# Three output buffers for narrowed weights, later routing gates, and the fixed-address token group last

## The chip, the cores and the metric

The kernel runs on one core of a Trainium2 chip. The time is the device time of one launch in microseconds (us), the median of three runs; the profile is of one further execution of the same program. The core's engines run side by side and meet through semaphores: PE multiplies matrices, DVE and ACT work on vectors, POOL does small vector work, and SP mostly issues DMA transfers. Each engine takes its instructions in the order in which they were written.

## The reference

Three layers run one after the other on 4 batches of 576 tokens, in float32:

```python
scores = scale * np.matmul(q, k.transpose(0, 1, 3, 2)) + bias      # 8 heads of 64
attn = exp(scores - max) / (sum + 1e-09)
x = (attn @ v) as [2304, 512]

e_idx = np.argmax(x @ w_gate, axis=1)                               # one of 8 experts per token
for e in range(E):                                                  # 512 -> 1024 -> 512
    out[mask] = gate_w * eom * (np.maximum(x[mask] @ w1[e], 0.0) @ w2[e])

g, val = x @ w_gate, x @ w_val                                      # 512 -> 1536
out = (g * sigmoid(g) * val) @ w_out                                # 1536 -> 512
```

## The kernel before

The program has three parts. In the first (to about 300 us) the attention of 16 units (four head pairs by four batches) fills the tiles `xT[0]` to `xT[3]`, each 128 rows by 2304 columns, one 576-column stretch per batch.

In the second (about 300 to 560 us) the expert layer is written as 64 steps, 16 per batch. Step n issues `h_step(n+1)` (12 matmuls, L590, evicted by ACT L592 and DVE L593), then `y_step(n)` (12 matmuls, L603, which read what L592 and L593 wrote), and then the side work that tables put at that step: `at(n, f)` and `after(n, f)` (L1047, L1086) collect it, and the loop at L1169 writes it out. An engine never overtakes, so side work that waits holds up whatever stands behind it on the same engine. Each batch is first run through its first expert; a packed list of leftover tokens then goes through one more expert. That list comes from the `q_` functions: `q_meta` (L624) loads the gate values of the chosen expert by DMA, `q_keep` (L640) marks tokens on DVE (L644 to L647), `q_rank` ranks them, `q_load` (L635) loads their `x` (L638), `q_tok` (L661) transposes it on PE (L666) and copies it on ACT (L667) into the buffer that held the layer's output `yo`. `QN` (L42) gives their steps. `x_save` (L617) writes a batch's `x` to DRAM (L619). The transfer `x<-yo` (L1142) writes a batch's result.

Side work also prepares the third layer's weights. They arrive as 64-bit values, and a "stash" reads one piece of 128x1024 words into one of three `xT` tiles (L982 or L984, three steps ahead), narrows it with one ACT instruction (L993) and three DVE instructions (L996, L999, L1002) into an output buffer in `xT[2]`, and stores it to the DRAM tensor `wn` (L1039). `NS` lists the steps of its 18 pieces, `NS2` those that spread over two steps.

In the third part (from about 560 us) the dense layer passes over three token groups of 768 columns, j = 0, 1, 2, in 12 steps each. Each pass ends with six result tiles o(h, m) of 128x512 in PSUM, copied to SBUF by DVE (L1552) or ACT (L1554) and sent to DRAM by SP (L1556). Two of the groups consist of batches whose numbers are only known at run time (`r0`, `r1`, `r2`), so their addresses are registers; the third (batch 3 and the last 64 tokens of every batch) has fixed addresses. The order of the groups is 0, fixed, 1 before the change. `ld_x` (L1471) loads the next group's input. SP's transfers count up eight semaphores in turn (DMAHW0 to 7 in the rows below), and a transfer waits for the one eight places earlier on its own semaphore. Two transfers to register addresses of the same DRAM tensor are also ordered by a wait, since the program cannot know that they do not overlap.

Of the kernel before, what the change touches and what calls it, by code (L numbers as in the profile page):

```python
# [13 lines left out]
AF = mybir.ActivationFunctionType  # L14
# [21 lines left out]
PR = {0: 72, 1: 73, 5: 75}  # L36
EB = 4
N0, NPL = 6, 6
NS = (9, 10, 13, 18, 19, 20, 21, 24, 25, 29, 34, 35, 37, 39, 40, 41, 43, 49)
NS2 = (13, 29, 37, 43)  # L40
RT = (3, 4, 5, 5, 6, 7, 7)
QN = (43, 46, 44, 46, 49, 54, 56)  # L42
EL, EC = ((47, 51, 53), (50, 51, 52, 53, 55, 56))
QT, SX = (44, 2)
SP0 = (10, 12, 14, 16, 17)
# [68 lines left out]
def body(tc, qt, kt, va, vb, ws, moe_w_gate, moe_w_output_gate, moe_w1, moe_w2, w_gate, w_val, w_out, ctab, cst, cst2, out):  # L114
    nc = tc.nc
    with ExitStack() as ctx:
# [39 lines left out]
        for r in range(4):  # L156
            o = slice(32 * r, 32 * r + 32)
# [7 lines left out]
        xT = {}  # L165
# [448 lines left out]
        def x_src(p, b):  # L614
            return xT[p][:, b * S:b * S + S]

        def x_save(b):  # L617
            for p in range(NP):
                nc.sync.dma_start(x1[p, :, b], x_src(p, b))  # L619
# [280 lines left out]
        for n, (ui, c) in enumerate(steps):  # L900
            p, b = units[ui]
# [28 lines left out]
            if old:  # L930
                x = pS.tile([128, 2, 512], F32, tag="S", name="Tx") if c == 4 else None
                t = t_pe(old[3], old[4], x, sts[ui - 1] if ui else None)
# [87 lines left out]
            return xT[(0, 1, 3)[i % 3]].bitcast(I32)[:, 0:1024]  # L1020

        def s_out(i):
            return xT[2][:, 512 * (i % 2):512 * (i % 2) + 512]

        def stash(i, n, m, two):

# [14 lines left out]
        def stash_ld(i, n, m):  # L1041
            at(m - 3, lambda: fetch_w(n, s_raw(i)))
# [43 lines left out]
        def at(n, *fs):  # L1086
            todo.setdefault(n, []).extend(fs)
        at(QN[0], q_meta)
        at(QT, lambda: xq.update(T=nc.values_load(lst[0:1, 64:65], min_val=0, max_val=28)))
# [3 lines left out]
        at(QY, lambda: x_first(1))  # L1093
        at(QN[1], q_load)
        at(QN[2], q_keep)
        at(QN[3], q_rank)
        for c in range(5):
            at(QN[4] + c, q_tok(c))
        at(QN[5], q_gather)
        at(QN[6], q_selt)  # L1100
        for i in range(N0 // 2):
            at(EL[i], lambda i=i: early_ld(i))
        for n in range(N0):
            for i, f in enumerate(early_cv(n)):
                at(EC[n] + i + (n == 3 and i == 2), f)
        for i, m in enumerate(NS):
            stash(i, 3 * NPL + i, m, m in NS2)
        for i, m in enumerate(NS):
            stash_ld(i, 3 * NPL + i, m)
# [11 lines left out]
            at(F1[f - 5], lambda f=f: m_load_f(0, f))  # L1121
        at(3, lambda: m_gate(0))
        for b in range(B):
            at((4, 5, 28, 30)[b], lambda b=b: x_save(b))
        for b in range(1, B):
            n = 16 * b - 15
            for i, f in enumerate(mu[b]["sp"]):
# [16 lines left out]
        a, z = prev  # L1144
        t = t_pe(a[3], a[4], None)
# [13 lines left out]
        t = t_pe(z[3], z[4], None)  # L1159
# [9 lines left out]
        for n in range(16 * B):  # L1169
            b, s = divmod(n, 16)  # L1170
# [204 lines left out]
        with ExitStack() as c2:  # L1375
# [140 lines left out]
            def rows(j, h, m):  # L1516

                def dst(b, c):
                    return of[bass.ds(b, 1) if not isinstance(b, int) else slice(b, b + 1), 0:512].rearrange("o (p c) d -> c p (o d)", c=4)[c]
                if j == 0:  # L1520
                    return [(0, 128, dst(r0, 2 * h + m) if m < 2 else dst(r1, h))]
                if j == 1:
                    return [(0, 128, dst(r2, 2 * h + m - 1) if m else dst(r1, 2 + h))]
                if m:
                    return [(0, 128, dst(3, 2 * h + m - 1))]
                return [(32 * b, 32, of[b, 512 + 32 * h:544 + 32 * h]) for b in range(B)]

            def outs(n, h, m):
                j, f = steps[n]
                first, last = n % NF == 0, n % NF == NF - 1  # L1530
                if first:
                    ops[h, m] = po.tile([128, 512], F32, tag=f"o{h}{m}", name="o")
                t = ops[h, m]
                uh, ul = (u[:, 128 * m:128 * m + 128] for u in sv[n]["u"][h])
                oh, ol = wt[f][2]
                for i, (u, w) in enumerate(((uh, oh), (uh, ol), (ul, oh))):
                    nc.tensor.matmul(t, u, w, start=first and i == 0, stop=last and i == 2)  # L1537
                if last:
                    end = j == 2
                    if end:  # L1540
                        o = sv["end"][:, 512 * (3 * h + m):512 * (3 * h + m) + 512]
                    else:
                        o = wp.tile([128, DM], F32, tag="ot", bufs=3, name="ot")
                    parts = rows((0, 2, 1)[j], h, m)
                    if end and (h, m) == (1, 2):
                        nc.vector.tensor_copy(o[:, 0:256], t[:, 0:256])  # L1546
                        nc.scalar.activation(o[:, 256:512], t[:, 256:512], AF.Copy)  # L1547
                        nc.sync.dma_start(parts[0][2][:, 0:256], o[:, 0:256])
                        nc.sync.dma_start(parts[0][2][:, 256:512], o[:, 256:512])
                        return  # L1550
                    if m % 2 == 0:
                        nc.vector.tensor_copy(o, t)  # L1552
                    else:
                        nc.scalar.activation(o, t, AF.Copy)  # L1554
                    for a, c, dst in parts:
                        nc.sync.dma_start(dst, o[a:a + c])  # L1556

            def it(n):

                N = len(steps)  # L1560
                j, f = steps[n] if n < N else (3, 0)
                i = n % NF
# [94 lines left out]
                F("h")  # L1657
                O(1, 2)
                if j < 2 and i == NPL + (j == 0):
                    ld_x(2 - j)  # L1660

            for n in range(6, 9):
                n_load(n)
# [23 lines left out]
```

## Time and profile before

| what | value |
|---|---|
| median of the runs shown (lowest to highest) | 992.91 us (992.63 to 994.26) |
| profiled execution: its own time, its span | 994.33 us, 992.4 us |
| PE busy, share of span | 953.1 us, 96% |
| DVE, ACT, POOL busy | 694.2, 532.0, 115.9 us |
| mean granted TensorE clock | 0.991 |
| moved by DMA, mean rate | 130.26 MB, 131 GB/s |

The span runs from the first to the last instruction; the execution's own time is 1.9 us longer. PE is the engine with least idle time, so what counts is where PE waits, where its clock was granted at half (1.2 instead of 2.4 GHz), and what follows its last matmul.

### The profile page before, as it was taken

How to read it: one execution, taken by the hardware profiler on the slowest of the kernel's cores; microseconds unless marked ns; L12 is line 12 of the kernel's file. 1: busy time of each engine (PE TensorE's matmuls, PEld its weight loads, DVE VectorE, ACT ScalarE, POOL GpSimd, SP SyncE). 2: the span in 40 equal slices, each digit the busy share in tenths (PEclk: the TensorE clock that was granted, in tenths of full speed). 3: DMA queues.
4: the chain of work that ended last, by engine and by line, in shares of the span. 5: the costliest groups of instructions: out<-in, count | busy, mean ns of one | idle time of the engine just before them, and what ended most of it. 6: DMA issues, size and time to landing. Idle time of an engine off the chain costs nothing. (4 is left out here: it accounts for less than half of the span.)

```text
span 992.4 us, 19678 instructions
## 1 busy us (share of the span) xinstructions
PE 953.1 (96%) x7633; PEld 813.4 (82%) x7633; DVE 694.2 (70%) x1548; ACT 532.0 (54%) x1125; POOL 115.9 (12%) x116
## 2 busy tenths in 40 slices
PE   7979999999999999999899999999999999999994
PEld 2337777777768999999899899999999999999993
DVE  8977888877786676677456577777556677367652
ACT  6778777777775343534335444554434455244441
POOL 2673434343300000000000000000000000000000
PEclk9999999999999999999999999999999999999997
DMA  6785334333044473947745585420312300312101
GB/s 203 206 258 172 124 92 130 97 114 112 2 143 154 144 266 121 373 150 234 252 135 200 169 258 180 118 75 1 127 32 84 109 33 22 107 53 75 64 1 64
DMA packets 90271, 130.26 MB, mean 131 GB/s; under 512 B 13728, under 2 KB 48032, under 8 KB 90176
## 3 DMA queue, kind: packets, MB, share of 16 engines
q1 hardware_dynamic: 90176, 128.99, 40.5%
q8 instruction: 60, 0.98, 0.4%
q14 instruction: 35, 0.29, 0.1%
HBM read 93.50 MB, written 35.46 MB: 130 GB/s over the span
## 5 line engine op out<-in xcount | busy, mean ns | idle before, releaser
L272 DVE CUSTOM_DVE_ANT_0 E<-S,bias 128x576 f32<-128x576 f32 x128 | 91.8, 755 | 31.2 <-PE S L268 25.1
L277 ACT ACTIVATE E<-E,st 128x576 f32<-128x576 f32 x144 | 110.3, 769 | 4.2 <-DVE st L272 3.9
L1275 PE MATMUL Y<-fv,ws 128*128 128x384 f32 x540 | 108.8, 336 | 0.1
L1275 PEld LDWEIGHTS Y<-fv,ws 128*128 128x128 f32 x540 | 95.7, 188 | 3.2 <-issue 0.4
L268 PEld LDWEIGHTS S<-kh,qz 64*128 64x128 f32 (+1 forms) x576 | 56.1, 185 | 39.2 <-DVE st L272 22.0
L379 PE MATMUL pv<-pt,rawv 128*64 128x320 f32 (+1 forms) x576 | 88.1, 422 | 0.0
L268 PE MATMUL S<-kh,qz 64*128 64x288 f32 (+1 forms) x576 | 82.0, 320 | 4.6 <-DVE st L272 3.4
L1537 PE MATMUL o<-ws,u 128*128 128x512 f32 x306 | 84.1, 394 | 0.0
L1016 DVE TENSOR_TENSOR ws<-r,ws 128x512 fp32r<-128x512 f32 (+1 forms) x66 | 51.4, 779 | 32.0 <-ACT ws L1013 31.1
L1275 PE MATMUL X<-fr,ws 128*128 128x384 f32 x360 | 73.3, 338 | 0.0
L592 ACT ACTIVATE qz<-T 128x288 fp32r<-128x288 f32 x63 | 25.8, 409 | 88.2 <-PE T L590 87.2
L318 ACT ACTIVATE pt<-T 128x512 f32<-128x512 f32 (+3 forms) x112 | 50.7, 467 | 38.6 <-PE T L295 38.2
L1275 PEld LDWEIGHTS X<-fr,ws 128*128 128x128 f32 x360 | 65.0, 188 | 5.6
L1537 PEld LDWEIGHTS o<-ws,u 128*128 128x128 f32 x306 | 56.2, 187 | 6.6 <-DVE u L1330 0.4
L603 PE MATMUL y<-qz,w2hl 128*128 128x288 f32 x384 | 57.8, 300 | 3.5 <-DVE qz L593 1.7
L603 PE MATMUL y<-qz,whl 128*128 128x288 f32 x384 | 56.9, 296 | 1.6 <-DVE qz L593 1.6
L320 DVE COPY pt<-T 128x512 f32<-128x512 f32 (+3 forms) x112 | 55.8, 522 | 3.3 <-PE T L295 3.1
L603 PEld LDWEIGHTS y<-qz,w2hl 128*128 128x128 f32 x384 | 53.7, 191 | 4.7 <-ACT qz L592 2.7
L590 PE MATMUL T<-xh,whl 128*128 128x288 f32 x256 | 57.1, 298 | 0.0
L590 PE MATMUL T<-xh,w1hl 128*128 128x288 f32 x248 | 55.7, 300 | 0.0
L295 PE MATMUL T<-ident,E 64*128 64x64 f32 x1248 | 54.5, 222 | 0.0
L603 PEld LDWEIGHTS y<-qz,whl 128*128 128x128 f32 x384 | 52.8, 188 | 2.1 <-DVE qz L593 2.1
(314 smaller groups left out, 2099.8 us busy)
## 6 DMA issues: line engine op xcount, KB each, us to landing
r<-wn SPq DMA_DIRECT2D x22, 512.0 KB, 3.5
bscr<-ob SPq DMA_DIRECT2D x36, 288.0 KB, 3.7
bias<-bscr SPq DMA_DIRECT2D x14, 576.0 KB, 4.3
raww<-in_moe_w_dram SPq DMA_DIRECT2D x10, 768.0 KB, 7.3
raww<-in_moe_w_dram SPq DMA_DIRECT2D x14, 512.0 KB, 5.8
raww<-in_moe_w_dram SPq DMA_DIRECT2D x22, 256.0 KB, 4.2
ro<-wn SPq DMA_DIRECT2D x22, 256.0 KB, 2.6
rawq<-in_qt_dram SPq DMA_DIRECT2D x16, 320.0 KB, 3.0
```

The costliest lines, as they stand in the source:

```text
L268: nc.tensor.matmul(t[:, f, 0:288], x[k, a], y[k, o], start=i == 0, stop=i == 2)
L272: nc.vector.tensor_tensor_reduce(out=E.rearrange("p (a b) -> p a b", a=2), in0=ps[:, :, 0:288], in1=bt[p, hh, c].rearrange("p (a b) -> p a ...
L277: nc.scalar.activation(E, E, AF.Exp, bias=st[:, 2 * c + hh:2 * c + hh + 1], scale=-1.0, accum_out=st[:, 10 + 2 * c + hh:11 + 2 * c + hh])
L295: nc.tensor.transpose(t[r][:, at:at + 64], E[k, o:o + 128], ident[k, k])
L318: nc.scalar.activation(o, x, AF.Copy)
L320: nc.vector.tensor_copy(o, x)
L379: nc.tensor.matmul(st["ps"][64 * hh:64 * hh + 64, 0:w], vt[p][:, hh, b, c, :], y, start=c == order[0], stop=c == order[4])
L590: nc.tensor.matmul(ps, wa[:, x, k], xs[k][y][:, o], start=k == 0 and i == 0, stop=k == 3 and i == 2)
L603: nc.tensor.matmul(hbuf["y"][d // 2][:, d % 2, 0:288], wb[:, x, d], t[:, y:y + 288], start=f == 0 and i == 0, stop=(one or f == 7) and i == 2)
L1016: return lambda: eng.tensor_tensor(l, t, h.bitcast(F32), ALU.subtract)
L1275: nc.tensor.matmul(bank, a[:, c], x[:, k], start=first and k == 0 and n == 0, stop=k == 1 and n == 2, skip_group_check=True)
L1537: nc.tensor.matmul(t, u, w, start=first and i == 0, stop=last and i == 2)
```

## The change

- The passes of the third part take the token groups in the order 0, 1, fixed: the `rows((0, 2, 1)[j], ...)` at L1544 becomes `rows(j, ...)`, and `ld_x(2 - j)` becomes `ld_x(j + 1)`.
- In the last pass DVE copies o(0,0), o(0,2), o(1,0) and o(1,1), and ACT copies o(0,1); before, DVE copied o(0,0), o(0,2), o(1,0) and ACT o(0,1), o(1,1). o(1,2) stays split in halves. The transfers of that pass go out partly on SP, partly on ACT: thirteen of them (eight of 32 rows), six on ACT.
- From piece 8 on, the stash takes three output buffers in turn, the third at columns 1152 to 1664 of `xT[2]`, where batch 2 lay.
- The stash list loses step 49 and gains step 26, so that pieces 9 to 17 move to an earlier place in the list.
- `x_save` of batches 2 and 3 stands at steps 22 and 33 (before 28 and 30).
- `q_keep` stands at step 45 (before 44).

```diff
-NS = (9, 10, 13, 18, 19, 20, 21, 24, 25, 29, 34, 35, 37, 39, 40, 41, 43, 49)
+NS = (9, 10, 13, 18, 19, 20, 21, 24, 25, 26, 29, 34, 35, 37, 39, 40, 41, 43)
-QN = (43, 46, 44, 46, 49, 54, 56)
+QN = (43, 46, 45, 46, 49, 54, 56)
...
         def s_out(i):
-            return xT[2][:, 512 * (i % 2):512 * (i % 2) + 512]
+            o = 512 * (i % 2) if i < 8 else (0, 512, 1152)[i % 3]
+            return xT[2][:, o:o + 512]
...
-            at((4, 5, 28, 30)[b], lambda b=b: x_save(b))
+            at((4, 5, 22, 33)[b], lambda b=b: x_save(b))
...
-                    parts = rows((0, 2, 1)[j], h, m)
+                    parts = rows(j, h, m)
                     if end and (h, m) == (1, 2):
                         nc.vector.tensor_copy(o[:, 0:256], t[:, 0:256])
                         nc.scalar.activation(o[:, 256:512], t[:, 256:512], AF.Copy)
                         nc.sync.dma_start(parts[0][2][:, 0:256], o[:, 0:256])
-                        nc.sync.dma_start(parts[0][2][:, 256:512], o[:, 256:512])
+                        nc.scalar.dma_start(parts[0][2][:, 256:512], o[:, 256:512])
                         return
-                    if m % 2 == 0:
+                    if (h, m) == (0, 1) or m == 1 and not end:
+                        nc.scalar.activation(o, t, AF.Copy)
+                    else:
                         nc.vector.tensor_copy(o, t)
-                    else:
-                        nc.scalar.activation(o, t, AF.Copy)
                     for a, c, dst in parts:
-                        nc.sync.dma_start(dst, o[a:a + c])
+                        act_q = end and ((h, m) == (0, 1) or a >= 96 - 32 * (h == 0))
+                        (nc.scalar if act_q else nc.sync).dma_start(dst, o[a:a + c])
...
-                    ld_x(2 - j)
+                    ld_x(j + 1)
```

On DVE, at steps 44 to 46, before (`meta` is the table that `q_meta` loads, `xT` the stash, `w1hl` and `w2hl` converted expert weights, `qz` the evicted h):

```order
L644 TENSOR_SCALAR meta<-meta,vm 128x5
L645 COPY meta<-meta 128x1
L647 TENSOR_TENSOR meta<-meta 128x1 x3
L1002 SCALAR_TENSOR_TENSOR xT_2758<-xT_1741,xT_2758 128x512
L553 TENSOR_TENSOR w1hl<-raww,w1hl 128x512
L553 TENSOR_TENSOR w2hl<-raww,w2hl 128x512
L593 SCALAR_TENSOR_TENSOR qz_117<-T,qz_117 128x288
```

and the same place after the change (line numbers are higher by one behind L1023 and by two behind L1556):

```order
L1002 SCALAR_TENSOR_TENSOR xT_2758<-xT_3776,xT_2758 128x512
L553 TENSOR_TENSOR w1hl<-raww,w1hl 128x512
L553 TENSOR_TENSOR w2hl<-raww,w2hl 128x512
L593 SCALAR_TENSOR_TENSOR qz_117<-T,qz_117 128x288
L644 TENSOR_SCALAR meta<-meta,vm 128x5
L645 COPY meta<-meta 128x1
L647 TENSOR_TENSOR meta<-meta 128x1 x3
```

The three `meta` rows moved behind one stash instruction, two conversions and one eviction L593.

On ACT, at steps 48 to 50, before (`tok` is the transposed leftover tokens, `whl` converted weights):

```order
L592 ACTIVATE qz_117<-T 128x288
L667 ACTIVATE tok<-qps 128x512
L993 ACTIVATE xT_2758<-xT_3776 128x512
L551 ACTIVATE whl<-raww 128x512 x2
L592 ACTIVATE qz_117<-T 128x288
```

and after:

```order
L592 ACTIVATE qz_117<-T 128x288
L667 ACTIVATE tok<-qps 128x512
L551 ACTIVATE whl<-raww 128x512 x2
L592 ACTIVATE qz_117<-T 128x288
L667 ACTIVATE tok<-qps 128x512
```

The stash instruction L993 is gone from between the copy of the tokens and the conversions; on DVE its three instructions are gone from the same step, and on SP its load (L984) no longer stands between `q_load` and `x<-yo`.

On SP, the last transfers of the program before, with the semaphores that each waits for:

```order
L1556 DMA out_dram<-oend 128x512 [waits DMAHW5_49,DVE_49]
L1556 ISA
L1556 DMA out_dram<-oend 128x512 [waits DMAHW7_49,DMAHW6_49,Activation_49]
L1548 ISA
L1548 DMA out_dram<-oend 128x256 [waits DMAHW7_49,DMAHW0_49,DVE_49]
L1549 ISA
L1549 DMA out_dram<-oend 128x256 [waits DMAHW1_49,DMAHW0_49,Activation_49]
```

and SP's share after, in the order o(0,0) twice, o(0,2), o(1,0) three times, o(1,1), left half of o(1,2):

```order
L1558 DMA out_dram<-oend 32x512 [waits DVE_49]
L1558 DMA out_dram<-oend 32x512
L1558 DMA out_dram<-oend 128x512 [waits DMAHW1_49,DVE_49]
L1558 DMA out_dram<-oend 32x512 [waits DMAHW3_49,DVE_49]
L1558 DMA out_dram<-oend 32x512 [waits DMAHW5_49]
L1558 DMA out_dram<-oend 32x512 [waits DMAHW6_49]
L1558 DMA out_dram<-oend 128x512 [waits DMAHW0_49,DVE_49]
L1549 DMA out_dram<-oend 128x256 [waits DMAHW1_49,DVE_49]
```

Before, each transfer waits for the one just before it. After, the waits on a DMAHW semaphore are for a transfer eight places earlier; the last one's, on DMAHW1, is for o(0,2).

On ACT at the same place after the change; before, no transfer stood on ACT:

```order
L1558 DMA out_dram<-oend 32x512 [waits DVE_49]
L1558 DMA out_dram<-oend 32x512
L1553 ACTIVATE oend<-o 128x512 [waits PE_49]
L1558 DMA out_dram<-oend 128x512 [waits Activation_49]
L1558 DMA out_dram<-oend 32x512 [waits DVE_49]
L1548 ACTIVATE oend<-o 128x256 [waits DVE_49]
L1550 DMA out_dram<-oend 128x256 [waits DMAHW7_49,Activation_49]
```

The first two transfers, pieces of o(0,0) that wait for DVE's copy, stand ahead of ACT's own copy of o(0,1).

## Rows read from the trace of the kernel before

**Rows 1.** Busy time by 25 us windows: window, length, five engines, PEclk, DMA, GB/s

```profile
475.00:500.00 25.00, 21.66 (x152) 20.93 (x151) 11.18 (x22) 9.44 (x19) 0.00 (x0) 0.93 0.66 230
...
950.00:975.00 25.00, 25.00 (x129) 22.77 (x128) 13.37 (x26) 9.74 (x21) 0.00 (x0) 1.00 0.00 1
```

**Rows 2.** The same by 5 us windows, 475 to 490 us

```profile
475.00:480.00 5.00, 4.59 (x36) 4.35 (x35) 0.06 (x1) 0.00 (x0) 0.00 (x0) 1.00 1.00 386
...
485.00:490.00 5.00, 4.63 (x24) 4.61 (x25) 2.40 (x5) 1.01 (x2) 0.00 (x0) 0.66 0.87 271
```

**Rows 3.** Timeline, steps 22 to 31: start, length, engine, line, idle before and releaser

```profile
379.04 0.38 SPq L984 DMA_DIRECT2D xT<-in_w_out_dram  x1
...
397.42 3.43 SPq L619 DMA_DIRECT2D x<-xT  x4
...
406.12 0.66 ACT L993 ACTIVATE xT<-xT 128x512 f32<-128x512 f32 x1 [2.82 <-DMA xT<-in_w_gate_dram]
...
409.60 1.75 PE L603 MATMUL y<-qz,whl 128*128 128x288 f32 x11 [0.26 <-DVE qz L593]
```

**Rows 4.** Timeline, steps 44 to 46

```profile
460.75 0.23 DVE L644 TENSOR_SCALAR meta<-meta,vm 128x5 f32<-128x5 f32 x1 [3.64 <-DMA meta<-gscr]
...
463.47 0.45 DVE L593 SCALAR_TENSOR_TENSOR qz<-T,qz 128x288 fp32r<-128x288 f32 x1
...
463.98 1.72 PE L603 MATMUL y<-qz,whl 128*128 128x288 f32 x11 [1.36 <-DVE qz L593]
```

**Rows 5.** Timeline, steps 47 to 51

```profile
467.89 2.48 SPq L638 DMA_DIRECT2D qz<-x  x4
...
476.48 0.33 PE L666 MATMUL qps<-ident,qz 128*128 128x128 f32 x1 [0.41 <-DMA qz<-x]
...
480.68 0.60 ACT L667 ACTIVATE tok<-qps 128x512 f32<-128x512 f32 x1 [6.10 <-DMA x<-yo]
481.17 0.66 ACT L993 ACTIVATE xT<-xT 128x512 f32<-128x512 f32 x1
...
483.22 0.40 PE L603 MATMUL y<-qz,w2hl 128*128 128x288 f32 x1 [1.18 <-ACT qz L592]
...
485.37 2.73 PE L603 MATMUL y<-qz,w2hl 128*128 128x288 f32 x11 [1.75 <-DVE qz L593]
```

**Rows 6.** DMA issues, 466 to 482 us: count, KB each, median us to landing

```profile
qz<-x SPq DMA_DIRECT2D x4, 288.0 KB, 3.9
x<-yo SPq DMA_DIRECT2D x1, 1152.0 KB, 9.6
xT<-in_w_out_dram SPq DMA_DIRECT2D x1, 512.0 KB, 7.3
```

**Rows 7.** Timeline, the end of the program

```profile
976.02 1.88 DVE L1552 COPY oend<-o 128x512 f32<-128x512 f32 x3
976.73 9.04 SPq L1556 DMA_DIRECT2D out_dram<-oend  x5
...
978.28 0.42 DVE L1546 COPY oend<-o 128x256 f32<-128x256 f32 x1 [0.38 <-PE o L1537]
978.74 0.38 ACT L1547 ACTIVATE oend<-o 128x256 f32<-128x256 f32 x1 [0.54 <-DVE oend L1546]
...
989.60 0.33 SPq L1549 DMA_DIRECT2D out_dram<-oend  x1
```

**Rows 8.** DMA issues, then waits of SP (total, times, longest), from 965 us

```profile
out_dram<-oend SPq DMA_DIRECT2D x5, 256.0 KB, 2.1
...
SPq L1556 <- DMA out_dram<-oend: 6.5, 4, 1.6
```

**Rows 9.** Timeline, the ends of the first and second pass

```profile
699.90 11.41 SPq L1556 DMA_DIRECT2D out_dram<-ot  x6
...
732.25 1.55 DVE L1009 TENSOR_TENSOR r<-r 128x256 f32<-128x256 f32 x4
...
838.54 9.62 SPq L1556 DMA_DIRECT2D out_dram<-ot  x12
```

## The prediction

> **What bounds the kernel now.** I read the windows by 25 us first. From 575 us to the last full window PE is busy throughout at full granted clock [rows 1]: in the third part the reader is to see that only PE's own work counts, and nothing that the change does to other engines there can be gained or lost until some wait outgrows its cover. Two things remain. The windows of the second part show one where PE is idle 3.3 us and the clock was granted at 0.93 [rows 1]; by 5 us windows the half clock sits at 485 to 490, with 0.66 [rows 2], directly behind two PE waits. And after the last matmul the span runs on for long. So I read, in this order, the timeline of PE's waits in the second part (each with its releaser, then what that releaser itself waited for), the DMA issues around the largest, and the timeline and SP's waits at the end.
>
> **The waits in the second part.** Four places, in order of time.
>
> Step 31: PE waits 0.26 us for DVE, which is late because ACT's stash L993 waited 2.82 us for its load; that load went out beside the four transfers of `x_save` for batch 2 (SP 397.42) and expert weights [rows 3]. The change issues these four right behind the load at 379.04 [rows 3], some 18 us earlier. I take the 0.26 as gained.
>
> Step 46: PE waits 1.36 us for DVE's L593 at 463.47. DVE had stood idle 3.64 us in front of `q_keep`, whose table landed at 460.75, with a stash instruction, two conversions and that L593 queued behind it [rows 4]. In the new order all four go ahead of `q_keep`, so they use up the idle 3.64 us, and PE's wait goes: 1.36. What is late next is `q_keep` itself: behind it now stand two conversions and the following L593, which runs for the y after the one that waited. PE reaches that y at least one y (1.72 us) [rows 4] after step 46's; the wait would come back only if the table landed over 1 us later than 460.75. Nothing in the change delays its issue, and SP's `x_save` has left its neighbourhood long before.
>
> Step 49: PE waits 0.41 us for the `q_load` transfers, issued at 467.89 [rows 5]. On SP they stand behind the loads of the last expert weights, which wait for a buffer that the conversions behind `q_keep` free. With those done before 460.75, `q_load` goes out some 4 us sooner and 0.41 goes.
>
> Step 51: PE waits 1.18 us for ACT and 1.75 us for DVE [rows 5]. ACT had idled 6.10 us in front of the token copy L667 until `x<-yo` landed at about 480.6; that transfer took 9.6 us for 1152 KB [rows 6] while the engines moved 386 GB/s [rows 2], with the 512 KB load of the stash of step 49 and the four `q_load` transfers in flight. In the new order that load does not exist there (512 KB at 386 GB/s: 1.4 us) and `q_load` is out of the way (4 x 288 KB: 3.0 us); `x<-yo` also starts 1.4 us earlier, since DVE is no longer late. What is left beside it are two 512 KB loads and a small one, 2.5 MB with itself: 6.4 us, against 9.6. So ACT copies at about 475.5 to 476, some 4 to 5 us earlier, and also no longer has L993 (0.66) behind it, nor DVE its three stash instructions. The two waits of 2.93 us lie within that. The half clock follows them; without idle time on PE I expect it to stay at 2.4 GHz: 5.0 x (1 - 0.66) = 1.7 us [rows 2].
>
> Sum: 0.26 + 1.36 + 0.41 + 2.93 + 1.7 = 6.66 us. Against it stand the added edits. The stash at step 26 puts one ACT and three DVE instructions in front of conversions that are wanted five steps later; the nearest row is step 31, where a stash beside conversions cost PE 0.26 [rows 3], so 0 to 0.3, or below nothing, since the same instructions leave step 49. The new third buffer must be free of `x_save` of batch 2, which is issued three steps before the first write; at the rate of [rows 2] its 1.2 MB take 3.1 us, so 0. `x_save` of batch 3 now stands on SP past a pair of stash loads and the gate load of step 32 and in front of the next load and two stores; its issue takes 3.43 us there [rows 3], and one stash may come late by that less its slack: 0 to 0.5. I take 0.4 for all three, so the second part gives 6.3 us, with ends at 1.6 (steps 31 and 46 alone) and 6.9.
>
> **The end of the passes.** The register-addressed chain of six transfers, 11.41 us on SP, moves from the last pass to the second, where twelve fixed ones took 9.62 [rows 9]. On SP the weight loads of the next pass stand behind it. After the first pass the chain already stands so: it begins at 699.90 and the weights are first touched at 732.25, so it has 32.3 us and needs 11.4 [rows 9]; PE shows no idle time there [rows 1]. The cover is 21 us: cost 0. The swapped input loads (ten transfers against four) lie under the same full PE: 0.
>
> **The tail.** Before: ACT's half ends at 979.12, and the span ends 13.3 us later. SP issues seven transfers from 976.73 to 989.60, 2.15 us apart [rows 7], since each waits for the one before (6.5 us in four of the waits), and one lands 2.1 us after its issue [rows 8]. After the change no transfer waits for its neighbour. DVE's copies follow each other every (1.88 - 0.68) / 2 = 0.60 us (one alone about 0.68, estimated from three in 1.88), so with a fourth copy the left half runs from 978.4 and ACT's half ends at about 979.25, 0.1 later than before [rows 7]. On SP two pieces of o(0,0) go at 976.73 and 977.1, o(0,2) at 977.45; the left half of o(1,2) waits for o(0,2) to land, 977.45 + 2.1 = 979.55, and its issue is the last. From the last issue to the end of the span it was 992.4 - 989.60 = 2.8 us, which gives 982.4. The transfers now share the engines: 1.5 MB in all, the first 256 KB landing at about 978.8, the rest at 386 GB/s needing 3.4 us, so 982.2, and 0.9 from landing to the end: 983.1. I take 983.2, a gain of 9.2. Ends: 982.0 (gain 10.4) if the sharing costs nothing and the semaphore comes early, 985.5 (gain 6.9) if small pieces run at the 271 GB/s of [rows 2] and the ACT queue, which no row shows, starts late. ACT's own copy of o(0,1) waits for DVE's copy and two issues, to about 977.45; only its transfer waits for it.
>
> The Trainium skill, "DMA: Bandwidth & Descriptors", section "Issuing engines are not separate DMA queues", says that transfers started on several engines run on the same 16 DMA engines, and that the second queue saves issue time alone. By it the six issues on ACT save SP at most 6 x 0.35 us and the tail ends at 983.1; if each queue had its own rate it would be 982.4. No run here shows a transfer from ACT yet.
>
> Total 9.2 + 6.3 = 15.5 us: the span 992.4 becomes 976.9, the profiled execution 994.33 becomes 978.8, and the median, 1.4 us below that execution, 992.91 becomes 977.4.
>
> **Rivals.**
>
> *The wait at step 51 only shrinks.* `x<-yo` still ends last, PE waits over a microsecond, and the clock is granted at half as before. For it: the engines are at their full rate there [rows 2], and a transfer shares them with whatever else is in flight. Against: 1.7 MB fewer beside it. Then 2.93 falls to about 1.5 and 1.7 stays: 977.4 + 3.2 = 980.6.
>
> *The tail frees itself by half.* The transfers collide, or ACT's queue starts slowly, and the end moves 5.5 us instead of 9.2. For it: thirteen transfers, eight of them small, where seven stood. Against: twelve fixed ones went out in 9.62 us with copies between them [rows 9]. 977.4 + 3.7 = 981.1.
>
> *More goes than counted.* The later half clock and idle time (before 575 us) go too, when everything ahead of them is earlier, and the tail reaches its best: 977.4 - 3.2 - 1.0, about 973.2.
>
> *Slower: the thirteen transfers take turns.* If at the end each transfer took a full turn of 2.15 us though nothing makes it wait, thirteen would need 13 x 2.15 = 28 us where seven took 15, and the tail would be 12.9 longer: 992.9 + 12.9 - 6.3 = 999.5. It decides from the tenth transfer in a row on, 7 x 2.15 + 6.3 = 21.4 us. Against: twelve transfers in 9.62 us [rows 9], which turns of 2.15 us exclude unless small pieces are dearer on ACT.
>
> **How the numbers follow.** The forecast 0.55, its own range 975.5 to 979.5; step 51 only shrinks 0.19; half the tail 0.11; more than counted 0.10; slower 0.02; something that eats the whole of it 0.03. The range 974.5 to 982 holds the forecast, most of the first two rivals and a little of the third. Below 0.2% (2 us) a measurement of this kernel cannot tell a change from none: faster 0.95, same 0.03, slower 0.02.
>
> **What the profile would show.** Right: the transfers of `oend` issued within some 3.5 us of each other on two queues, and under 5 us from ACT's half to the end of the span; no PE wait before L603 at steps 46 and 51; DVE busy in front of L644; the token copy L667 about 5 us earlier and no half clock near 485; the third part unchanged, without PE idle time behind the second pass. Wrong: an issue of `oend` that waits 1.6 us for its neighbour; L667 still behind `x<-yo` with PE waiting; a new PE wait around steps 25 to 35, where `x_save` and the stash moved; or SP's weight loads arriving late after the second pass.

## The result: 980.52 us, 13 us less, and the profile after

| | kernel before | changed kernel |
|---|---|---|
| median (lowest to highest) | 993.59 us (992.63 to 997.87, 4 runs) | 980.52 us (977.00 to 982.68, 4 runs) |
| ratio | | 0.9857, 95% interval 0.9812 to 0.9902 |
| median of a second measurement | 995.00 us (992.11 to 998.99, 13 runs) | 980.38 us (976.84 to 981.77, 5 runs) |
| its ratio | | 0.9840, interval 0.9814 to 0.9866 |
| profiled execution: own time, span | 994.33 us, 992.4 us | 982.68 us, 980.8 us |
| mean granted clock of it | 0.991 | 0.991 |

The ratios are not quotients of the two medians, which would be 0.9868 and 0.9853. One execution of a kernel below, e4_keep, took 1035.53 us at a mean clock of 0.856 and is left out of its figures. The forecast was 977.4 us, a ratio of 0.9844 to the 992.91 us then known. The span of the profiled execution fell by 11.65 us. Cut at points that both traces have (first y matmul of a step, first matmul of the third part, last matmul, end), it went here:

| stretch | before | after | change |
|---|---|---|---|
| start to step 0 (attention) | 301.32 | 304.77 | +3.45 |
| step 0 to step 31 | 107.73 | 107.73 | 0.00 |
| step 31 to step 46 | 53.28 | 53.53 | +0.25 |
| step 46 to step 52 | 28.19 | 20.92 | -7.27 |
| step 52 to the third part | 73.44 | 73.49 | +0.05 |
| third part to the last matmul | 414.28 | 414.28 | 0.00 |
| last matmul to the end | 14.19 | 6.05 | -8.14 |

So two stretches gave 15.4 us and 0.3 were lost beside them, 15.1 net against 15.5 forecast for the whole; a further 3.45 us were lost in the first part, whose code is the same in both kernels.

The window of the changed kernel over steps 47 to 51, and the last full one (columns as in [rows 1]):

```profile
475.00:500.00 25.00, 25.00 (x191) 24.37 (x190) 10.87 (x20) 9.56 (x19) 0.00 (x0) 1.00 0.71 238
950.00:975.00 25.00, 24.72 (x124) 21.86 (x122) 13.18 (x24) 8.70 (x17) 0.00 (x0) 1.00 0.04 9
```

The 3.3 us of idle PE and the 0.93 of [rows 1] are gone. The 0.28 us of the second row is the last matmul's end at 974.72.

Steps 45 to 51 in its timeline, which answer to [rows 4, 5] (the first PE row is step 46, the last step 51):

```profile
464.55 0.23 DVE L644 TENSOR_SCALAR meta<-meta,vm 128x5 f32<-128x5 f32 x1 [0.60 <-DMA meta<-gscr]
...
466.03 1.75 PE L603 MATMUL y<-qz,whl 128*128 128x288 f32 x12
...
466.88 2.47 SPq L638 DMA_DIRECT2D qz<-x  x4
...
472.79 0.40 SPq L1143 DMA_DIRECT2D x<-yo  x1
...
477.66 0.60 PE L666 MATMUL qps<-ident,qz 128*128 128x128 f32 x4
...
478.37 0.60 ACT L667 ACTIVATE tok<-qps 128x512 f32<-128x512 f32 x1 [1.73 <-DMA x<-yo]
...
483.31 1.79 PE L603 MATMUL y<-qz,w2hl 128*128 128x288 f32 x12
```

No PE row has a bracket: steps 46, 49 and 51 run their twelve (or four) matmuls in one piece where before the rows split at a wait. DVE's idle time in front of `q_keep` is 0.60 us where it was 3.64, and ACT's in front of the token copy 1.73 us where it was 6.10. `x<-yo` landed 5.6 us after its issue (472.79 to 478.37) instead of 9.6 [rows 6]. From step 46 (466.03) to `q_load` it is now 0.85 us, and was 5.56.

Step 31 and what leads to it, after, for [rows 3]:

```profile
400.43 0.61 SPq L982 DMA_DIRECT2D xT<-in_w_val_dram  x1
...
409.83 0.66 ACT L993 ACTIVATE xT<-xT 128x512 f32<-128x512 f32 x1 [3.07 <-DMA xT<-in_w_val_dram]
...
413.31 1.75 PE L603 MATMUL y<-qz,whl 128*128 128x288 f32 x11 [0.51 <-DVE qz L593]
```

The same wait stands there, 0.51 us instead of 0.26, and ACT's L993 still waits for its load. (The pieces have moved up one place in the list, so that this load is of `w_val` now and was of `w_gate` in [rows 3].)

The end of the program, after, for [rows 7]:

```profile
972.50 2.48 DVE L1555 COPY oend<-o 128x512 f32<-128x512 f32 x4
973.21 3.42 SPq L1558 DMA_DIRECT2D out_dram<-oend  x7
973.22 0.88 ACTq L1558 DMA_DIRECT2D out_dram<-oend  x2
974.14 0.60 ACT L1553 ACTIVATE oend<-o 128x512 f32<-128x512 f32 x1 [2.15 <-PE o L1538]
974.77 0.87 ACTq L1558 DMA_DIRECT2D out_dram<-oend  x2
974.89 0.42 DVE L1547 COPY oend<-o 128x256 f32<-128x256 f32 x1
975.68 0.38 ACT L1548 ACTIVATE oend<-o 128x256 f32<-128x256 f32 x1 [0.95 <-DVE oend L1547]
976.10 0.38 ACTq L1550 DMA_DIRECT2D out_dram<-oend  x1
976.74 0.41 SPq L1549 DMA_DIRECT2D out_dram<-oend  x1
```

Thirteen transfers go out in 3.9 us (973.21 to 977.15) on two queues, where seven took 13.2 us. Eight stand on SP and five on ACT; the six on ACT that the description of the change and the prediction count are one too many. SP issues seven of its eight without a pause, 0.49 us each (3.42 / 7), and these end 0.1 us before the eighth, the left half of o(1,2), begins. The issues, for [rows 8] (count, KB each, median us to landing):

```profile
out_dram<-oend SPq DMA_DIRECT2D x2, 256.0 KB, 3.5
out_dram<-oend SPq DMA_DIRECT2D x5, 64.0 KB, 1.9
out_dram<-oend ACTq DMA_DIRECT2D x1, 256.0 KB, 3.3
```

The 3.5 us of the first row are those of o(1,1), issued at 976.17. The other transfer of that row is o(0,2), issued third, at 974.12; in the trace its semaphore's count is complete at 976.61, 2.5 us after its issue. So a transfer of 256 KB lands 2.5 to 3.5 us after its issue, where it took 2.1 alone.

The pass ends, after, for [rows 9], then PE in the 25 us behind the second:

```profile
696.39 11.52 SPq L1558 DMA_DIRECT2D out_dram<-ot  x6
...
835.02 11.53 SPq L1558 DMA_DIRECT2D out_dram<-ot  x6
```
```profile
850.00:875.00 25.00, 25.00 (x130) 23.15 (x129) 11.68 (x22) 9.49 (x19) 0.00 (x0) 1.00 0.12 47
```

The chain of register-addressed transfers stands behind both passes now, and PE shows no idle time behind it.

### The profile page after: what moved, and what is told of

The parts are those of the page before. It is cut to its first block, busy times and chain, and to the rows that moved or that the text cites. A ratio compares the mean times of both kernels' runs of the same rounds, so it can differ in the third digit from the quotient of the medians.

```text
span 980.8 us, 19674 instructions
## 1 busy us (share of the span) xinstructions
PE 954.5 (97%) x7633; PEld 814.9 (83%) x7633; DVE 695.1 (71%) x1549; ACT 531.8 (54%) x1124; POOL 116.2 (12%) x116
## 5 line engine op out<-in xcount | busy, mean ns | idle before, releaser
L268 PE MATMUL S<-kh,qz 64*128 64x288 f32 (+1 forms) x576 | 84.0, 325 | 3.8 <-DVE st L272 2.4
L295 PEld LDWEIGHTS T<-ident,E 64*128 64x128 f32 x1248 | 53.1, 142 | 2.5 <-issue 1.1
```

The source lines that it names most:

```text
L268: nc.tensor.matmul(t[:, f, 0:288], x[k, a], y[k, o], start=i == 0, stop=i == 2)
L295: nc.tensor.transpose(t[r][:, at:at + 64], E[k, o:o + 128], ident[k, k])
```

## The experiments

All have the kernel before as their base unless said otherwise; ratios are to the runs of before on the same chip (995.41 us in the median beside e1 to e4, 995.00 beside e5, after_again, e6 and e7, 996.11 beside e8 and e9, and a single 993.79 beside the single run of e10). "Steps 46 to 52" and "tail" are measured as in the table above.

| run | median us | ratio, 95% interval | PE waits at 31 / 46 / 49 / 51 | steps 46 to 52 | tail |
|---|---|---|---|---|---|
| before | | | 0.26 / 1.36 / 0.41 / 2.93 | 28.19 | 14.19 |
| after | 980.52 | 0.9857 [0.9812, 0.9902] | 0.51 / 0 / 0 / 0 | 20.92 | 6.05 |
| e1_tail | 986.98 | 0.9909 [0.9879, 0.9938] | 1.99 / 0.67 / 0.33 / 2.94 | 27.33 | 5.95 |
| e2_order | 986.84 | 0.9915 [0.9884, 0.9945] | 0.20 / 0.70 / 0 / 2.57 | 24.90 | 7.27 |
| e3_second | 987.87 | 0.9936 [0.9913, 0.9959] | 0.20 / 0 / 0 / 0 | 20.92 | 14.18 |
| e4_keep | 989.97 | 0.9938 [0.9915, 0.9961] | 1.62 / 0 / 0 / 0 | 21.07 | 14.19 |
| e5_stash | 989.45 | 0.9947 [0.9924, 0.9971] | 1.02 / 1.34 / 0 / 0 | 22.52 | 14.20 |
| after_again | 980.38 | 0.9840 [0.9814, 0.9866] | 0.97 / 0 / 0 / 0 | 20.92 | 6.22 |
| e6_merge | 987.09 | 0.9923 [0.9897, 0.9948] | 0.18 / 0 / 0 / 0 | 20.93 | 12.10 |
| e7_load | 985.76 | 0.9908 [0.9886, 0.9929] | 0 / 0 / 0 / 0 | 20.93 | 12.39 |
| e8_balance | 979.83 | 0.9831 [0.9804, 0.9858] | 0 / 0 / 0 / 0 | 20.92 | 5.87 |
| e9_nostash | 980.27 | 0.9841 [0.9815, 0.9867] | 0 / 0 / 0 / 0 | 21.00 | 5.79 |
| e10_half | 985.32 (one run) | | 1.54 / 0 / 0 / 0 | 20.93 | 4.99 |

**The two halves apart.** e1_tail takes the third part of the change alone, e3_second the second part alone (lists, buffer, `x_save`, `q_keep`), e2_order only the order of the groups:

```diff
-                    parts = rows((0, 2, 1)[j], h, m)
+                    parts = rows(j, h, m)
...
-                    ld_x(2 - j)
+                    ld_x(j + 1)
```

> Before plus the end of the program as changed: group order, copies and transfers; the second part as before. Theory (the two gains add): PE's last matmul stands where it stood in before, apart from the granted clock, and from there to the end of the span it is 6.1 us as in the changed kernel, against 14.2 before: 8.1 us less. Rival (part of the tail's gain comes from transfers that run elsewhere earlier): the stretch stays over 7 us. Second rival (the half clock seen at 73 and 281 us in the changed kernel comes from its use of a second transfer queue): it is there in each run of this kernel, and in none of before.

> Before plus the new group order alone; copies as before and all thirteen last transfers on SP. Theory (what goes is the wait of each transfer for the one before): the thirteen are issued back to back at 0.35 to 0.5 us each, and last matmul to end of span takes 7 to 8 us, 1 to 1.5 us more than with two queues. Rival (the sharing of queues carries the gain, since transfers of one queue take turns of 2 us): the stretch stays over 11 us.

> Before plus the edits of the second part alone: stash list, third buffer, x_save steps, q_keep step. Theory: step 52 starts 7 us earlier than in before, with no PE wait at steps 46, 49 and 51, the half clock near 485 us gone, and a wait of 0.3 to 0.5 us left at step 31; last matmul to end of span 14.2 us as before. Time about 7 us less, more or less by the half clock of the first part. Rival (the tail's relief helps the second part or the other way round): step 52 gains less than 6 us.

By ratio the tail alone gives 0.9 per cent (9.1 us of 995) and the second part alone 0.6 (6.4 us); together 15.5 us, beside the 15.9 us of after_again. In the profiles it is 8.2 and 7.3, and the intervals, 2 to 3 us to each side, hold both. So the theories of e1_tail (of the tail) and of e3_second (of step 52 and the tail) held. The figure of the second part depends on the execution it is taken from: the same second part took 28.19 us in the profile of before, 27.33 in e1_tail and 24.90 in e2_order, and with all edits 20.92 or 20.93 in each, so that its gain lies between 4.0 and 7.3 us. e2_order keeps all transfers on SP:

```profile
975.39 5.09 SPq L1556 DMA_DIRECT2D out_dram<-oend  x11
...
980.58 0.40 SPq L1548 DMA_DIRECT2D out_dram<-oend  x1
981.08 0.41 SPq L1549 DMA_DIRECT2D out_dram<-oend  x1
```

Its eleven first transfers leave every 0.46 us, none waits for its neighbour, and the tail is 7.27 us. So the order alone brings 6.9 of the 8.1 us, and the second queue, together with DVE's copy of o(1,1), another 1.2.

e2_order also separates waits from clock at step 51. The windows of steps 46 to 52 in before, e2_order and after, one row each:

```profile
462.33:490.52 28.19, 23.49 (x163) 22.55 (x161) 16.43 (x36) 9.73 (x20) 0.00 (x0) 0.94 0.78 255
```
```profile
465.31:490.21 24.90, 21.63 (x162) 20.95 (x161) 15.78 (x34) 9.76 (x20) 0.00 (x0) 1.00 0.79 271
```
```profile
466.03:486.95 20.92, 20.92 (x162) 20.92 (x161) 12.74 (x29) 9.45 (x19) 0.00 (x0) 1.00 0.88 297
```

Idle PE is 4.70, 3.27 and 0 us. e2_order, with the same second part as before, has a wait of 2.57 us at step 51 and a granted clock of 1.00 behind it, where before had the half clock (1.2 GHz) for 3.4 us. PE's busy time of 23.49, 21.63 and 20.92 us then says: 1.86 us for the half clock, and 0.71 us more busy time around three waits without it. Matmul ends are modelled in the profile, so whether the matmuls there take longer or the wait itself is longer than its bracket says is not shown.

**Which edit undoes step 51.** e4_keep moves `q_keep` alone, e5_stash takes the stash list, third buffer and `x_save` without it:

```diff
-QN = (43, 46, 44, 46, 49, 54, 56)
+QN = (43, 46, 45, 46, 49, 54, 56)
```

> Before plus q_keep one step later, alone. Theory (q_keep's wait is the root: it delays the weight loads and q_load on SP, and these x<-yo): step 47 starts 1.6 us earlier, the 0.4 us wait at step 49 goes, x<-yo lands some 3 us sooner, and of the 2.9 us at step 51 less than 1 us is left, without half clock; step 52 gains 5 to 6.5 us. Rival (the stash of step 49 is the root of step 51): step 47 gains 1.6 us and step 49 0.4, but 1.5 us or more of the wait at step 51 stays with the half clock; step 52 gains about 2 to 3 us.

> Before plus the stash list, the third buffer and the x_save steps; q_keep stays at step 44. After the run with q_keep alone took away nearly all of the second part's gain, theory: q_keep is the root of the waits at steps 46, 49 and 51, and the stash list only shortens what is left; then step 47 starts no earlier than in before (wait of 0.7 to 1.4 us at step 46), and step 51 keeps 0.5 to 2 us of its 2.9. Rival (either edit alone removes the jam at step 51): no PE wait at step 51, step 52 gains about 4 us.

Timeline of e4_keep:

```profile
463.15 0.22 DVE L644 TENSOR_SCALAR meta<-meta,vm 128x5 f32<-128x5 f32 x1
...
465.32 1.75 PE L603 MATMUL y<-qz,whl 128*128 128x288 f32 x12
...
468.24 0.43 SPq L984 DMA_DIRECT2D xT<-in_w_out_dram  x1
...
472.08 0.40 SPq L1142 DMA_DIRECT2D x<-yo  x1
...
478.09 0.60 ACT L667 ACTIVATE tok<-qps 128x512 f32<-128x512 f32 x1 [2.15 <-DMA x<-yo]
```

and of e5_stash:

```profile
463.27 0.23 DVE L644 TENSOR_SCALAR meta<-meta,vm 128x5 f32<-128x5 f32 x1 [3.68 <-DMA meta<-gscr]
...
466.50 1.75 PE L603 MATMUL y<-qz,whl 128*128 128x288 f32 x11 [1.34 <-DVE qz L593]
...
470.37 2.46 SPq L638 DMA_DIRECT2D qz<-x  x4
473.25 0.40 SPq L1143 DMA_DIRECT2D x<-yo  x1
...
480.92 0.60 ACT L667 ACTIVATE tok<-qps 128x512 f32<-128x512 f32 x1 [3.86 <-DMA x<-yo]
```

`q_keep` alone takes away every wait from 46 to 51 though the 512 KB load of step 49 is still there: that load now goes out 3.8 us ahead of `x<-yo` instead of 0.53 (470.41 and 470.94 in before), because `q_load`, which stands before it on SP, is no longer late. The transfer then takes 5.9 us. Step 52 gains 7.1 us, more than the 5 to 6.5 of its theory. Taking the load away without moving `q_keep` leaves `q_load` directly ahead of `x<-yo`, which takes 7.7 us, enough for PE, but the 1.34 us at step 46 stay. So the theory of e5_stash fell (no wait is left at step 51) and its rival held: either edit is sufficient at step 51, only `q_keep` helps at 46. The prediction had reckoned with the removed load and the earlier `q_load` together.

**The stash edits put back.** e9_nostash is e8_balance (below) with the old stash list, two buffers and the old `x_save` steps, `q_keep` at 45, and one early load:

```diff
-NS = (9, 10, 13, 18, 19, 20, 21, 24, 25, 26, 29, 34, 35, 37, 39, 40, 41, 43)
+NS = (9, 10, 13, 18, 19, 20, 21, 24, 25, 29, 34, 35, 37, 39, 40, 41, 43, 49)
...
-            o = 512 * (i % 2) if i < 8 else (0, 512, 1152)[i % 3]
-            return xT[2][:, o:o + 512]
+            return xT[2][:, 512 * (i % 2):512 * (i % 2) + 512]
...
-            at(m - (5 if i == 10 else 3), lambda: fetch_w(n, s_raw(i)))
+            at(m - (5 if i == 9 else 3), lambda: fetch_w(n, s_raw(i)))
...
-            at((4, 5, 22, 33)[b], lambda b=b: x_save(b))
+            at((4, 5, 28, 30)[b], lambda b=b: x_save(b))
```

> The kernel of the run beside it, but with the stash list, the two output buffers and the x_save steps of the kernel before (step 49 back, step 26 out, x_save at 28 and 30); q_keep stays at step 45, the early load is that of the piece before step 31. Theory: q_keep alone undoes the waits of steps 46, 49 and 51, so the other three edits of the second part add nothing: steps 47 to 52 take 17.3 to 17.6 us as in the run beside it, steps 25 to 46 take the same within 0.5 us, and the two times agree within 0.5 us (0.05%). Rival: the stash of step 49 still costs; PE waits again 0.5 us or more between steps 47 and 52, or x_save at 28 and 30 beside the loads costs 0.5 to 2 us around step 31, and the kernel is 0.5 to 2 us slower than the run beside it.

980.27 against 979.83 us, from the same step 0 to step 52 in 181.44 against 181.35: the theory held. Beside `q_keep` and an early load, the third buffer, the list and the `x_save` steps are worth nothing that shows.

**Run to run.** after_again is the changed kernel itself, without an edit.

> The changed kernel once more. Theory (the half clock of the first part comes and goes between executions of the same program): spans spread over some 5 us and fall as the mean granted clock rises, about 5 us for each 0.005 to 0.006 of mean clock in this kernel and in before alike; from the start of step 0 to step 31 nothing but the granted clock and the wait at step 31 differs. Rival (the changed kernel always has the half clock near 73 and 281 us): it is there again at the same places.

The changed kernel came out at 980.38 us with a wait of 0.97 at step 31. Its profile has the half clock near 73 us again (3.4 us from 66.3, 6.8 us from 73.1) and none near 281, so one of the two places came back and one did not; from step 0 to step 31 it took the same 107.73 us. Over all profiles with that load three steps ahead, step 31 waits 0.26, 1.99, 0.20 and 1.62 us with the old `x_save` (before, e1, e2, e4), and 0.51, 0.97, 0.20, 1.02, 0.18 and 1.54 with the new one (after, after_again, e3, e5, e6, e10). The place of `x_save`, which moved together with the stash list in all these, makes no difference there that can be seen. What the wait hangs on is the load, which in after took 9.3 us beside loads of expert weights, six of them of 512 to 768 KB, and three stores:

```profile
raww<-in_moe_w_dram SPq DMA_DIRECT2D x4, 512.0 KB, 6.4
raww<-in_moe_w_dram SPq DMA_DIRECT2D x2, 768.0 KB, 9.5
...
xT<-in_w_val_dram SPq DMA_DIRECT2D x1, 512.0 KB, 9.3
```

In before, with the four transfers of `x_save` issued right behind it, it took as long:

```profile
xT<-in_w_gate_dram SPq DMA_DIRECT2D x1, 512.0 KB, 9.3
```

**Merged transfers and the early load.** e6_merge is the changed kernel with the four 32-row pieces of o(0,0) and of o(1,0) sent as one transfer each, seven in all, three on ACT, with both halves of o(1,2) copied by DVE and o(1,1) by ACT; e7_load adds the early load of stash piece 10:

```diff
-                return [(32 * b, 32, of[b, 512 + 32 * h:544 + 32 * h]) for b in range(B)]
+                return [(0, 128, of[:, 512 + 32 * h:544 + 32 * h])]
...
-            at(m - 3, lambda: fetch_w(n, s_raw(i)))
+            at(m - (5 if i == 10 else 3), lambda: fetch_w(n, s_raw(i)))
```

> The changed kernel with each row of four 32-row transfers made one (seven transfers in place of thirteen), ACT copying and sending o(0,1) and o(1,1), and DVE copying both halves of o(1,2). Theory (the tail fell short of its forecast by the issue time of SP and ACT): the last issue stands about 0.9 us behind the last matmul in place of 2.0, and from the last matmul to the end it is 3.8 to 4.9 us in place of 6.05. Rival (the bytes set it, since all transfers share the DMA engines): it stays at 5.5 to 6.1 us.

> As the merged version, and the load of stash piece 10 goes out two steps earlier (step 24), ahead of the expert weights of batch 2. Theory (the wait at step 31 comes from this load standing behind weights on the queue, whatever x_save does): ACT no longer waits about 3 us for it at step 29, and PE's wait at step 31 is gone (0.2 to 2.0 us in the runs so far). Rival (the wait at step 31 comes from the weights themselves): ACT waits for weights in its place, and PE still waits at step 31 or 32.

The early load did what was expected: L993 finds its data and step 31 has no wait. The merge failed: the last issue stands 0.8 us behind the last matmul, as its theory had it, but the tail went back to 12.1 and 12.4 us, which neither theory nor rival allowed. Timeline of e6_merge, then its packets and issues:

```profile
971.51 2.04 SPq L1549 DMA_DIRECT2D out_dram<-oend  x1
971.85 1.74 ACTq L1550 DMA_DIRECT2D out_dram<-oend  x1
```
```profile
DMA packets 984, 1.57 MB, mean 58 GB/s; under 512 B 88, under 2 KB 344, under 8 KB 984
...
out_dram<-oend ACTq DMA_DIRECT2D x2, 256.0 KB, 9.2
```

Of its packets 88 are under 512 B, the semaphore writes: five transfers of 128 rows with 16 each and two merged ones with 4 each make 88, where sixteen for each would make 112. So a merged transfer, whose address has batches as its outermost dimension, ran on four of the sixteen engines, and what was queued behind it on those four landed 9 to 10 us after its issue. That fits the Trainium skill, "DMA: Bandwidth & Descriptors", section "Why a DMA increments its semaphore by 16 and not by 1", by which the number of engines is the largest up to 16 that divides the slowest dimension of both sides. The eight small transfers of the change are the better form: e8_balance (below) has the copies and the early load of e7_load with the small transfers, and a tail of 5.87 us instead of 12.39.

**What sets the new tail.** e8_balance is the changed kernel with the early load, DVE copying both halves of o(1,2) and ACT o(1,1), and the transfers shared anew:

```diff
-                        nc.scalar.activation(o[:, 256:512], t[:, 256:512], AF.Copy)
+                        nc.vector.tensor_copy(o[:, 256:512], t[:, 256:512])
...
-                    if (h, m) == (0, 1) or m == 1 and not end:
+                    if m == 1:
...
+                        if end and a >= 64:
+                            pend.append((dst, o[a:a + c]))
...
```

> The changed kernel with two further edits. One: the weights of stash piece 10 are loaded at step 24 instead of 26. Two: in the last pass DVE copies both halves of o(1,2), ACT copies o(0,1) and o(1,1), and ACT sends o(0,1), then the fixed-address pieces of o(0,0) that begin at row 64 or later, then o(1,1), the like pieces of o(1,0), and the right half of o(1,2); SP sends the rest. Theory: the tail of the changed kernel (6.05 us from the last matmul to the end of the span) is set by the bytes still to be moved when the last transfer is issued, 2.02 us behind the last matmul; the two queues issue as many transfers as before in about the same time, so the tail is 5.5 to 5.9 us, the wait in front of step 31 (0.51) is gone, and the kernel takes 0.5 to 1 us less than the changed one. Rival: the issues set the tail; with ACT free of the last copy the last issue comes 1 us sooner, the tail is 4.8 to 5.2 us, and the kernel takes 1.3 to 1.8 us less. Either way under 0.2%, so the profile has to tell, not the median.

e10_half is the changed kernel with as many transfers but 0.92 MB instead of 1.57:

```diff
-                        (nc.scalar if act_q else nc.sync).dma_start(dst, o[a:a + c])
+                        w = 256 if end else 512
+                        (nc.scalar if act_q else nc.sync).dma_start(dst[:, 0:w], o[a:a + c, 0:w])
```

> The changed kernel, whose last pass sends only the left 256 columns of each transfer but the two halves of o(1,2): as many transfers on the same queues, 0.92 MB instead of 1.57 MB; the right half of the other five result tiles of that pass is not written. Theory: the tail of 6.05 us is set by the bytes on their way, 1.57 MB at about 300 GB/s, and the last issue waits for o(0,2), which lands late because the engines are shared; with 0.65 MB less the tail is shorter by 1 to 2 us, 4.1 to 5.1 us. Rival: the number of transfers and their issue set it; then the tail stays within 0.3 us of 6.05.

In e8_balance the last issue came only 0.15 us earlier, where the rival had 1 us: it went to ACT, 1.87 us behind the last matmul at 973.36, and the tail is 5.87, as the theory had it (5.95 to 6.22 in the three profiles with the change's own end, after, after_again and e1_tail).

```profile
405.82 0.67 ACT L993 ACTIVATE xT<-xT 128x512 f32<-128x512 f32 x1
...
411.67 1.75 PE L603 MATMUL y<-qz,whl 128*128 128x288 f32 x12
...
975.23 0.41 ACTq L1550 DMA_DIRECT2D out_dram<-oend  x1
```

The first two rows are step 31 without its wait. In time e8_balance is 979.83 us, its interval overlapping that of the changed kernel: not shown to be faster. In e10_half the tail fell to 4.99 us, its last issue being 1.76 us behind the last matmul (978.44):

```profile
976.92 3.18 SPq L1559 DMA_DIRECT2D out_dram<-oend  x7
980.20 0.38 SPq L1549 DMA_DIRECT2D out_dram<-oend  x1
```

So 0.65 MB cost 1.06 us: 0.26 in an earlier last issue (1.76 instead of 2.02 us) and 0.80 behind it. That is at the lower edge of what the theory expected, and the rival fell. But the last issue did not wait for o(0,2), as the theory had it: in both kernels it stands 0.1 us behind SP's seven issues, which took 3.18 us here and 3.42 in after. The other 5 us stay with three fifths of the bytes; the time from the last issue to the end is still 3.2 us (4.0 in after), against 2.8 before with nothing else in flight.

## Why the prediction was right, and where it was off

*Steps 46, 49 and 51* (1.36 + 0.41 + 2.93 + 1.7 = 6.4 us): shown, 7.27 us against the profile of before (4.0 to 7.3 over the three profiles with the old second part). All the waits went, the token copy came 6.0 us earlier as counted from step 46 (forecast 4 to 5), `x<-yo` took 5.6 us (forecast 6.4), DVE filled its idle time in front of `q_keep` and `q_load` went out 4.7 us sooner (forecast 4). The term for the clock was right (1.86 by e2_order's rows, 1.7 forecast); 0.71 us came on top, which PE's rows around the waits are busy beyond the waits. What the prediction had wrong is the share: it took the removed load for one of the causes that were needed. e4_keep shows that `q_keep` alone gives 7.1 of the 7.27 us, since it also sends `q_load` and that load earlier and further ahead of `x<-yo`. At step 49 an earlier `q_load` was not needed either: in e5_stash it goes out 5.5 us behind step 46, as in before, and PE does not wait, nor did it in e2_order. The rival that step 51 only shrinks fell.

*Step 31* (0.26): this step failed. The wait was 0.51. The prediction read `x_save` of batch 2 as what held the load up, since it stood beside it; the runs with the old and the new place have the same scatter, and the load took 9.3 us with `x_save` behind it and without. The expert weights, named in the same sentence, are the largest of what is left beside it, which is argued and not shown by a run of its own; moving the load two steps earlier removed the wait, moving `x_save` did not.

*The added edits* (0.4 against): 0.0 from step 0 to 31 and +0.25 from 31 to 46, which is step 31's own wait. The stash at step 26 and the third buffer cost nothing that shows.

*The pass ends* (0): right. From the third part's first matmul to the last one the two kernels agree within 0.01 us, and all profiles lie at 414.24 to 414.29 us but that of e9_nostash (414.48).

*The tail* (9.2): the mechanism was right, the size was 8.14. Transfers no longer wait for their neighbour, which e2_order shows by itself. The mis-sized term is the last issue: forecast at 979.55, 1.3 us behind the last matmul, it came 2.02 us behind it; and from there to the end it took 4.0 us instead of 983.2 - 979.55 = 3.65. The prediction let the last issue wait for o(0,2) to land, which by its figures would have been the later event. In the trace it is held by SP itself: the seven issues before it take 0.49 us each, not the 0.36 that stand between the prediction's 976.73, 977.1 and 977.45, and end at 976.63; o(0,2) had landed at 976.61, itself 2.5 us behind its issue and not 2.1. In e10_half o(0,2) landed at 979.77, 0.43 us before the last issue, which again directly followed SP's chain. So the price of an issue is the term that was too small, and the landing, too small as well, would have put the last issue at about the same time in the changed kernel. By the rule of the Trainium skill, "DMA: Bandwidth & Descriptors", section "Issuing engines are not separate DMA queues", the second queue saves issue time alone. The trace agrees: between e2_order and the changed kernel, in which the last issue ends 4.6 and 2.4 us behind the last matmul, 2.2 us of issuing were saved, about what five issues cost at e2_order's 0.46. The tail gained 1.2 of them, since the last issue then has 4.0 us to the end instead of 3.1. The bound of 6 x 0.35 us had one issue too many and each too cheap. The rival of thirteen turns of 2.15 us fell: they left in 3.9 us. So did the rival of half the tail (5.5 us).

*The total.* 7.3 + 8.1 - 0.3 = 15.1 us against 15.5: the second part gave 0.7 more than forecast and the tail 1.1 less, and that these nearly cancel is luck. The profiled execution's span is 3.9 us above the forecast of 976.9; 3.45 of that lie elsewhere, in the first part, where the granted clock differs. That the median's 3.1 us above the forecast have the same source fits, but only profiled executions show it. The window there in before, and in after:

```profile
70.00:80.00 10.00, 7.68 (x115) 6.41 (x111) 7.18 (x18) 7.41 (x18) 0.24 (x1) 1.00 0.81 252
```
```profile
70.00:80.00 10.00, 8.81 (x87) 7.59 (x87) 5.74 (x15) 5.95 (x15) 0.00 (x0) 0.66 0.77 230
```

The profiled changed kernel has 6.8 us at half clock here and 3.4 us more from 281 us on, and reaches step 0 3.45 us later. Executions of it differ accordingly: 977.00 us at a mean clock of 0.999 and 976.84 at 1.000, 982.68 at 0.991. The first two lie at the forecast. Before differs too (992.02 at 0.989 to 999.50 at 0.982). The instructions of this stretch are the same in all kernels here. The half clock stood near 72 us also in kernels without a transfer on ACT (e2_order, e4_keep, e5_stash), and in none of this stretch in e3_second and e6_merge, so it does not come from ACT's queue; with what it goes stays open. Whether the change itself makes it likelier was not tried beyond these runs: ten of the twelve other profiles have it, the single one of before has none.

## What to carry to other kernels

When a late instruction on one engine holds back the transfers behind it, look for the earliest wait of the chain first: here one step's shift of a five-instruction group on DVE undid four waits, a half clock and a collision of transfers, and the edits that aimed at the collision itself added nothing beside it. At the end of a program, give the last transfers addresses that the program can tell apart, and count what the issuing queue needs: the last issue here stood behind seven others on SP, 3.42 us, and not behind a landing. Splitting rows into several small transfers can beat one transfer with a short outermost dimension.

## What was not expected of the hardware

- One transfer with an outermost dimension of 4 ran on 4 engines, and it slowed the others too: two 128 KB issues behind it took 2.04 and 1.74 us instead of about 0.4, and the tail 12.1 us instead of 6.05.
- The same instructions ran at 2.4 or 1.2 GHz from execution to execution: 2.57 us of PE waits at step 51 were followed by full clock in e2_order, 2.93 us by half clock in before, and 1.71 us near 545 us by half clock in some profiles (after) and not in others (e3_second).
- Steps with waits took longer than the waits in the profile's brackets: 0.71 us beyond the 3.27 us of three waits at full clock (e2_order), of which the modelled ends of matmuls may be a part.
